# A first block of 128 rows on half a batch, and mirrored rows added on VectorE in three batches

## The chip, the cores and the metric

One core of one Trainium2 chip runs the whole program. The metric is the time of one execution in device microseconds. The inputs, the weights and the result lie in the chip's memory; nothing is kept from one execution to the next.

## The reference, cut to what matters

Eight batches of 2496 tokens with 256 features go through a two-dimensional Fourier transform of which only the real part is kept. Each transformed token is then routed to one of eight experts, a two-layer network, and is scaled with its gate.

```python
X = np.fft.fft(np.fft.fft(x, axis=1), axis=2).real      # (8, 2496, 256)
x = X.reshape(19968, 256)
logits = x @ w_gate + modality_bias[modality_id]
e_idx = argmax(logits, 1); gate_w = softmax(logits)[e_idx]
for e in range(8):
    h = maximum(x[e_idx == e] @ w1[e], 0)               # 256 -> 1024
    out[e_idx == e] = gate_w * (h @ w2[e])              # 1024 -> 256
```

## The kernel before, in words

**The transform of a batch.** The host lays out each batch as a tile XM in two halves (c = 0 and 1) of five blocks each, and every half holds a plain part (`XM[:, 0]`) and a mirrored part (`XM[:, 1]`); what the transform needs is the sum of the two. Stage 1 (`stage1`, L539 in the batches below) multiplies XM with the constants c1, stage 2 (L570) with the matrices m2u, stage 3 (L585) with e3. Batches 0 to 2 run this in float32, where one matmul stands in the trace as two records; batches 3 to 7 run it in pairs of float16 (L536, L565, L583). Stages 2 and 3 are one generator, `stage23`, of twelve steps. Its results go from PSUM into rows `rp` (ScalarE L516, VectorE L517), and the columns for the gate go into Lg (L593).

**How the mirrored part gets in.** From batch 3 on VectorE adds the two parts first (`fold_add`, L397). In batches 0 to 2 (UB = 3) no add is made: stage 1 has two matmuls for each block, one with the plain and one with the mirrored part, and both add up in PSUM (L539). The sum of squares, from which a power of two for scaling is taken, then needs four passes on ScalarE in a batch (L394) where two would do with the sum (L398).

**Routing.** `route` picks the experts with some twenty small VectorE instructions, counts tokens on TensorE (L669, L671) and makes the row numbers `dsti` (L682). The rows go into a buffer `xd` in the chip's memory, sorted by expert: 11 indirect DMAs of plain rows (`rp`, called plus in the code) and 11 of mirrored rows (`rm`, VectorE L227 and L228) per batch, all issued by GpSimd (L708) one after the other.

**Expert blocks.** `block` takes 256 rows of one expert: SyncE reads the start row from a table (L1064), loads the rows transposed (xT, L1077) with their gates and row numbers (ig, L1080), then come 48 matmuls with w1 (L1096), ScalarE and VectorE into H (L1101, L1102), 48 matmuls with w2 (L1116), ScalarE into `ob` (L1124), and a scatter to the result on GpSimd (L1125). The first GEMM of a block runs ahead of the second GEMM of the block before it. Three lists of blocks with experts fixed in advance (ORDER_S) come first: experts 0, 1, 2 once batch 0 is scattered (`spec_blocks(ORDER_S[0], 1)`), then 13 blocks once batch 1 is scattered, then 8 once batch 2 is. A table on VectorE (`spec_table`) gives the start row, or empty rows where an expert has too few tokens. The other blocks follow from tables, and the last ones have 128 rows.

**Weights.** Each expert has two units of weights, w1 (even) and w2 (odd), 1 MB each. A unit is loaded (`wload`, L826), folded on VectorE if it is w1 (L834, L835), measured (L848 on TensorE), split into a high half on ScalarE (`whi`, L869) and a low half on VectorE (`wlo`, L876), and stored for later (`wstore`, L883). Units 0 to 5 are called by hand between steps of the batches, in the main function.

**What sets the order.** The program is written as generators that are stepped by hand (`steps`, `ORDER0`, `ORDER1`, SPOS). A scheduler then gives each engine one fixed order by priority: what is written earlier comes first unless its inputs are late by the scheduler's own clock; then later work is pulled ahead. `issue_after(x)` places an instruction behind x, `behind(f, x)` does so at lower priority, and `high_priority` pulls ahead. Each engine and each queue then runs in its fixed order, so an instruction that waits holds up everything behind it.

Of the kernel before, what the change touches and what calls it, by code (L numbers as in the profile page):

```python
# [22 lines left out]
P = 128  # L23
# [50 lines left out]
UB = 3  # L74
RV = 1
FG = 6
ORDER_S = (0, 1, 2), (0, 1, 2, 3, 3, 4, 4, 5, 5, 6, 6, 7, 7), (5, 6, 7, 0, 1, 2, 3, 4)
# [166 lines left out]
class Kernel:  # L244
# [116 lines left out]
    def scatter_dep(self, ins, b):  # L361
# [24 lines left out]

    def fold_add(self, b, c):
        n = 4 if b < UB else 2
        if c == 0:
            self.sq = self.fft.tile([P, n], F32, name=f"nst{n}")  # L390
        if b < UB:
            jk = self.wp.tile([P, NH * D], F16, name="xj", bufs=1)
            for h in range(2):
                self.nc.scalar.activation(jk.rearrange("p (i d) -> p i d", i=NH), self.XM[c][:, h], AF.Square, accum_out=self.sq[:, 2 * c + h:2 * c + h + 1])  # L394
# [60 lines left out]
    def scale(self, b):  # L455
# [7 lines left out]
        self.pow2(self.total(self.sq, self.psf.tile([P, 512], F32, name="psf")), eb, s, 204 if b >= FB else 188, 2.0 if b < UB else 1.0)  # L463
# [8 lines left out]
    def fold(self, b, c):  # L472
# [11 lines left out]
        if b < UB:  # L484
            self.PQ = self.XM[c][:, :, :, 0:P], self.XM[c][:, :, :, P:D]
# [33 lines left out]
    def stage1(self, b, c):  # L519
# [3 lines left out]
        for h, src in enumerate(self.PQ):  # L523
# [3 lines left out]
            for i0, n in ((0, 3), (3, 2)):  # L527
# [4 lines left out]
                for i in range(n):  # L532
# [4 lines left out]
                    elif b < UB:  # L537
                        for k in range(2):
                            self.staged = nc.tensor.matmul(o, src[:, k, i0 + i, :], self.c1[:, i1 + i, :], start=k == 0, stop=k == 1).ins  # L539
                    else:  # L540
                        nc.tensor.matmul(o, src[:, i0 + i, :], self.c1[:, i1 + i, :], start=True, stop=True)
# [83 lines left out]
    def route(self, b):  # L625
# [49 lines left out]
        V.tensor_tensor(nbase, ps[:, 176:184], self.base, ALU.add)  # L675
        self.base = self.bases[b + 1] = nbase
# [17 lines left out]
        for i, group in enumerate(groups):  # L694
            if b < 2:
# [3 lines left out]
                for x in group.list:  # L699
                    self.scatter(*x)  # L700
# [6 lines left out]
    def scatter(self, row, at, b):  # L707
# [3 lines left out]
        self.scatter_dep(i, b)  # L711
# [31 lines left out]
    def stream(self):  # L743
# [13 lines left out]
        for b in range(B):  # L757
# [4 lines left out]
            for g, _ in enumerate(self.stage23(b)):  # L762
# [3 lines left out]
                if g == 0 and b + 1 == FB:  # L766
                    self.m2_split()
# [5 lines left out]
                yield self.at(b)  # L773
            if b + 1 == FB:
# [545 lines left out]
```

## Time and profile before

| | us |
|---|---|
| median of 3 runs (lowest to highest) | 1033.86 (1032.04 to 1037.51) |
| the profiled execution, its own time | 1035.88 |
| its span, first to last instruction | 1034.1 |
| busy TensorE / VectorE / ScalarE / GpSimd | 1000.7 / 540.5 / 443.5 / 367.6 |

The profiled execution is 2.0 above the median, and 1.8 of it lie outside the span. TensorE is busy for 97% of the span, so the time is its work plus some 33 us in which it waits, and about half of that lies in the first 200 us, where the change is.

### The profile page before, as it was taken

Reading aid. Unit: us, or ns where it says so; the run is one execution under the profiler, and the core shown is the slowest. Engines: PE = TensorE matmul, PEld = TensorE weight load, DVE = VectorE, ACT = ScalarE, POOL = GpSimd, SP = SyncE. Lnnn points to the kernel's source line nnn. Section 1 sums busy time; section 2 is a strip of 40 time slices with the busy share of each in tenths; the row PEclk is TensorE's granted clock in tenths of the full one; section 3 lists DMA queues with packets and bytes.
Section 4 is the critical chain, followed back from the end, with each engine's and each line's share of the span. In section 5 each row is a group of like instructions: output and inputs, shape, how many; then the busy total and the mean of one; then the engine's idle time right before and its main releaser. Section 6 shows DMA issues by size and latency. Waiting matters only on the chain.

```text
span 1034.1 us, 25844 instructions
## 1 busy us (share of the span) xinstructions
PE 1000.7 (97%) x9910; PEld 904.4 (87%) x9910; DVE 540.5 (52%) x1577; ACT 443.5 (43%) x870; POOL 367.6 (36%) x351
## 2 busy tenths in 40 slices
PE   6989899999999999999999999999999999999996
PEld 6878788898998889999999998888888888889896
DVE  2859866576857558779754347423232322222221
ACT  4775566555643354455533333333232323233232
POOL 0077822135414441744344334335351212121111
PEclk9999999999999999999999999999999999999999
DMA  9837969278558958989766963897788895594891
GB/s 327 332 137 234 363 167 287 58 236 249 166 139 284 321 157 236 287 250 304 233 182 200 248 184 76 260 262 241 174 235 235 255 257 175 159 294 137 225 207 35
DMA packets 149725, 227.65 MB, mean 220 GB/s; under 512 B 116309, under 2 KB 117375, under 8 KB 132695
## 3 DMA queue, kind: packets, MB, share of 16 engines
q1 hardware_dynamic: 133031, 183.75, 61.1%
q0 software_dynamic: 16560, 42.15, 11.8%
q8 instruction: 80, 1.31, 0.5%
q14 instruction: 54, 0.44, 0.2%
HBM read 191.77 MB, written 62.48 MB: 246 GB/s over the span
## 4 chain that ended last, share of the span: by engine, by line
PE 69%; issue 12%; DMA 10%; POOL 4%; DVE 2%; ACT 2%; SPq 1%; POOLq 0%; ACTq 0%
PE psm L1096 30%; PE pso L1116 30%; DMA wa<-w 5%; DMA XM<-x 3%; POOL out L1125 3%; PE psf L565 2%; PE psf L583 2%; PE psf L570 2%; PE psf L536 1%; POOL xd L708 1%; PE psf L585 1%; DMA pack<-c_pack 1%; PE psf L539 1%; DMA xT<-xd 1%; DVE w L876 1%
## 5 line engine op out<-in xcount | busy, mean ns | idle before, releaser
L1096 PE MATMUL psm<-xT,w 128*128 128x256 f16 (+1 forms) x4368 | 454.4, 261 | 10.2 <-DVE H L1102 5.8
L1116 PE MATMUL pso<-w,H 128*128 128x256 f16 x3864 | 450.5, 273 | 0.9 <-ACT ob L1124 0.9
L1096 PEld LDWEIGHTS <-w 128*128 128x128 f16 x4368 | 384.3, 98 | 49.9 <-issue 8.4
L1116 PEld LDWEIGHTS <-H 128*128 128x128 f16 x3864 | 375.3, 98 | 43.7 <-issue 1.1
L1102 DVE SCALAR_TENSOR_TENSOR H<-psm,H 128x512 f16<-128x512 f32 x322 | 219.8, 687 | 334.6 <-ACT H L1101 334.0
L1125 POOL DMA_INDIRECT out<-ob,ig x161 | 164.7, 1023 | 516.9 <-ACT ob L1124 486.8
L1101 ACT ACTIVATE H<-psm 128x512 f16<-128x512 f32 x322 | 190.5, 596 | 229.9 <-PE psm L1096 227.1
L1124 ACT ACTIVATE ob<-pso,gs 128x256 f32<-128x256 f32 x161 | 68.6, 471 | 247.0 <-PE pso L1116 207.5
L708 POOL DMA_INDIRECT xd<-rp,dsti x88 | 101.4, 1152 | 94.3 <-DVE rm L228 49.9
L708 POOL DMA_INDIRECT xd<-rm,dsti x88 | 92.9, 1055 | 41.9 <-issue 18.5
L517 DVE SCALAR_TENSOR_TENSOR T<-psf,T 120x280 f16<-120x280 f32 (+2 forms) x95 | 43.4, 463 | 42.3 <-ACT T L516 42.2
L876 DVE SCALAR_TENSOR_TENSOR w<-wa,wsc,w 128x1024 f16<-128x1024 f32 x32 | 39.9, 1276 | 9.4 <-ACT w L869 9.3
L516 ACT ACTIVATE T<-psf 120x280 f16<-120x280 f32 (+2 forms) x95 | 38.8, 422 | 10.5 <-PE psf L536 5.7
L570 PE MATMUL psf<-m2u,T 128*120 128x280 f32 x132 | 37.2, 403 | 2.2 <-DVE Lg L593 1.5
L539 PE MATMUL psf<-c,XM 128*128 128x132 f32 x240 | 31.5, 294 | 7.0 <-DMA c<-c_c 6.9
L539 PEld LDWEIGHTS psf<-c,XM 128*128 128x128 f32 x240 | 30.4, 204 | 7.1 <-DMA XM<-x 6.9
L583 PE MATMUL psf<-T,pack 120*128 120x145 f16 x330 | 34.7, 224 | 1.5 <-DVE T L517 1.5
L869 ACT ACTIVATE w<-wa,wsc 128x1024 f16<-128x1024 f32 (+1 forms) x24 | 33.4, 1425 | 4.3 <-DVE wsc L405 3.5
L565 PE MATMUL psf<-pack,T 128*120 128x144 f16 (+1 forms) x330 | 31.5, 229 | 0.0
L512 ACT COPY T<-psf 120x280 f32<-120x280 f32 (+2 forms) x57 | 22.7, 407 | 17.1 <-PE psf L570 8.2
L855 ACT ACTIVATE xj<-wa 128x1024 f16<-128x1024 f32 x20 | 21.1, 1054 | 18.0 <-DVE wa L834 9.1
L516 ACT ACTIVATE rp<-psf 128x256 f16<-128x256 f32 x55 | 21.1, 383 | 15.8 <-PE psf L583 11.8
(186 smaller groups left out, 598.0 us busy)
## 6 DMA issues: line engine op xcount, KB each, us to landing
w<-w SPq DMA_DIRECT2D x80, 1028.0 KB
w<-w SPq DMA_DIRECT2D x80, 1024.0 KB
XM<-x SPq DMA_DIRECT2D x14, 1280.0 KB
wa<-w SPq DMA_DIRECT2D x16, 1024.0 KB
out<-ob,ig POOLq DMA_INDIRECT x161, 7.1
XM<-x SPq DMA_DIRECT2D x2, 768.0 KB
xT<-xd SPq DMA_TRANSPOSE x91
xd<-rp,dsti POOLq DMA_INDIRECT x88, 5.2
```

What stands on the lines that cost most here:

```text
L516: self.acted = self.nc.scalar.activation(dst[:, 0], ps, AF.Identity, scale=scale).ins
L539: self.staged = nc.tensor.matmul(o, src[:, k, i0 + i, :], self.c1[:, i1 + i, :], start=k == 0, stop=k == 1).ins
L565: nc.tensor.matmul(oh, T1[h][:, a, g, :], self.m2h[h][:, w], start=h + k == 0, stop=h * k == 2, skip_group_check=True)
L570: nc.tensor.matmul(ps[0:120, 0:280], T1[h][:, g, :], self.m2u[h], start=h == 0, stop=h == 1)
L583: nc.tensor.matmul(ps3[0:P, cols], self.e3h[:, a, j, :], T2[:, w, cols], start=k == 0, stop=k == 2)
L708: i = self.nc.gpsimd.indirect_dma_start(out=self.t["xd"], out_offset=bass.IndirectOffsetOnAxis(ap=at, axis=0), in_=row, in_offset=None, bo ...
L1096: l1 = nc.tensor.matmul(ps[:, q, :], w1v[:, h, kt, ft], xT[:, xs, :], start=k == 0, stop=k == 5).ins
L1101: nc.scalar.activation(H[:, 0, f0:f0 + NF, :], ps, AF.Relu)
L1102: self.mark = V.scalar_tensor_tensor(H[:, 1, f0:f0 + NF, :], ps, 0.0, H[:, 0, f0:f0 + NF, :], ALU.max, ALU.subtract).ins
L1116: nc.tensor.matmul(po[:, tg, :], H[:, hh, ft, tg * P:(tg + 1) * P], w2v[:, wh, ft, :], start=k == 0, stop=k == 23)
L1124: self.ob = nc.scalar.activation(ob, po[:, tg, :], AF.Identity, scale=gs[:, tg:tg + 1]).ins
L1125: ins = nc.gpsimd.indirect_dma_start(out=t["out"], out_offset=bass.IndirectOffsetOnAxis(ap=ig.bitcast(I32)[:, tg, 0:1], axis=0), in_=ob, i ...
```

## The change

It has six parts.
1. The mirrored half is added on VectorE in batches 0 to 2 too: batch 0 in four pieces as the data come (PARTS), batches 1 and 2 in two adds that are placed behind steps 7 and 9 of the `stage23` of the batch before (ADDS). Stage 1 then has one matmul for a block and the sum of squares two passes.
2. A block of 128 rows of expert 0 is run on the plain rows of batch 0 alone (HALF, `spec_table` with R = 0.5), after the first half of stage 1 of batch 2; it doesn't wait for mirrored rows (group xd_m0).
3. The first list has blocks of 128 rows, experts 0, 1, 1, 2, 2 where it had 0, 1, 2 of 256.
4. `whi`, `wlo`, `wstore` of unit 1 and the load of unit 5 come after routing of batch 0.
5. `m2_split` (the float16 copies of m2) moves from the `stage23` of batch 2 to behind that of batch 0.
6. Squares of both halves of batches 1 and 2 are called together at step f.

```diff
+ADDS = 7, 9
+HALF = (0,)
-ORDER_S = (0, 1, 2), (0, 1, 2, 3, 3, 4, ...
+ORDER_S = (0, 1, 1, 2, 2), (0, 1, 2, 3, 3, 4, ...
...
-        tc.add_to_no_dep_group(f"xd_w{b}", i)
+        tc.add_to_no_dep_group("xd_m0" if mirrored and b == 0 else f"xd_w{b}", i)
...
-        for b in range(self.nread, B):
+        if self.nread < 1:
+            tc.declare_no_dep(i, group="xd_m0", reason="only the plain rows are read")
+        for b in range(math.ceil(self.nread), B):
...
+    def add(self, c, *parts):
+        for i0, i1 in parts or ((0, NH),):
+            X = self.XM[c][:, 0, i0:i1]
+            self.nc.vector.tensor_tensor(X, X, self.XM[c][:, 1, i0:i1], ALU.add)
...
     def fold_add(self, b, c):
...
-        if b < UB:
-            jk = self.wp.tile([P, NH * D], F16, name="xj", bufs=1)
-            for h in range(2):
-                self.nc.scalar.activation(jk..., self.XM[c][:, h], AF.Square, ...)
-            return
         X = self.XM[c][:, 0]
-        self.nc.vector.tensor_tensor(X, X, self.XM[c][:, 1], ALU.add)
+        if b >= UB:
+            self.add(c)
+        elif b == 0:
+            self.add(c, *PARTS)
         self.nc.scalar.activation(self.XM[c][:, 1], X, AF.Square, accum_out=self.sq[:, c:c + 1])
...
-                    elif b < UB:
-                        for k in range(2):
-                            self.staged = nc.tensor.matmul(o, src[:, k, i0 + i, :], self.c1[:, i1 + i, :], ...)
                     else:
-                        nc.tensor.matmul(o, src[:, i0 + i, :], self.c1[:, i1 + i, :], start=True, stop=True)
+                        self.staged = nc.tensor.matmul(o, src[:, i0 + i, :], self.c1[:, i1 + i, :], ...).ins
...
+        if b == 0:
+            hb = rt.tile([1, 8], F32, name="hbase", bufs=1)
+            V.tensor_tensor(hb, ps[0:1, 8 * G:8 * G + 8], self.base[0:1, :], ALU.add)
+            self.bases[0.5] = hb
...
-                if g == 0 and b + 1 == FB:
-                    self.m2_split()
+                if b + 1 < UB and g in ADDS:
+                    with self.tc.issue_after(self.mark):
+                        self.add(ADDS.index(g))
...
+            if b == 0:
+                with self.tc.issue_after(self.acted), self.tc.issue_after(self.mark):
+                    self.m2_split()
...
-    behind(both(k.whi, 0, 1), k.acted)
-    behind(both(k.wlo, 0, 1))
-    both(k.wstore, 0, 1)()
-    both(k.wload, 4, 5)()
+    behind(both(k.whi, 0), k.acted)
+    behind(both(k.wlo, 0))
+    k.wstore(0)
+    k.wload(4)
     steps(12 - WHI)
     steps(7)
+    behind(both(k.whi, 1), k.expi)
+    behind(both(k.wlo, 1), k.plused, k.head)
+    k.wstore(1)
+    k.wload(5)
...
     steps(5)
+    k.hold = k.staged,
+    run_all([k.spec_blocks(HALF, 0.5, S=P)])
+    run_all([k.prev])
+    k.prev = None
     steps(3 + 1)
...
-    spec = k.spec_blocks(ORDER_S[0], 1)
+    spec = k.spec_blocks(ORDER_S[0], 1, S=P)
```

## Rows read from the trace of the kernel before

**Rows 1.** Windows of two stages: length, busy time (instructions) per engine, clock, DMA.
```profile
41.27:85.63 44.36, 40.88 (x341) 36.15 (x340) 31.61 (x158) 33.16 (x62) 23.94 (x23) 1.00 0.51 173
85.63:136.30 50.67, 46.00 (x364) 39.22 (x363) 42.65 (x112) 30.32 (x61) 42.49 (x27) 0.97 0.89 309
```

**Rows 2.** Windows of L539 alone (stage 1, batches 0, 1, 2): PE, PEld, clock, DMA.
```profile
6.90:18.84 11.94, 11.94 (x80) 11.78 (x80) 1.00 0.98 332
41.27:51.70 10.43, 10.00 (x80) 9.36 (x80) 1.00 0.93 333
75.18:85.63 10.45, 9.38 (x80) 9.04 (x80) 1.00 0.29 81
```

**Rows 3.** Timeline of PE: start, length, instructions [idle before, releaser].
```profile
18.84 0.52 PE L334 MATMUL psf<-awm,pack 128*128 128x16 f32 x4
...
21.75 0.63 PE L848 MATMUL psm<-wa 128*128 128x128 bf16 x8 [0.99 <-DVE wa L834]
22.23 2.09 PE L570 MATMUL psf<-m2u,T 128*120 128x280 f32 x8
...
38.46 0.75 PE L585 MATMUL psf<-T,pack 120*128 120x145 f32 x4 [0.37 <-ACT T L512]
...
61.58 1.17 PE L570 MATMUL psf<-m2u,T 128*120 128x280 f32 x4 [1.45 <-DVE Lg L593]
...
136.30 4.09 PE L1096 MATMUL psm<-xT,w 128*128 128x256 f16 x36 [1.13 <-DMA xT<-xd]
```

**Rows 4.** Groups by form of L397 and of L1096 with 256 and 128 columns.
```profile
L397 DVE TENSOR_TENSOR XM<-XM 128x1280 f32<-128x1280 f32 x10 | 14.9, 1488 | 15.6 <-DMA XM<-x 15.5
...
L1096 PE MATMUL psm<-xT,w 128*128 128x256 f16 x3360 | 394.7, 273 | 7.5 <-DVE H L1102 5.8 <-DMA xT<-xd 1.7
L1096 PE MATMUL psm<-xT,w 128*128 128x128 f16 x1008 | 59.7, 219 | 2.7 <-DMA w<-w 2.7
```

**Rows 5.** Timeline of VectorE.
```profile
50.20 0.18 DVE L682 CAST dsti<-dst 128x22 int32<-128x22 f32 x1
...
53.70 1.21 DVE L834 TENSOR_TENSOR wa<-wa 128x1024 f32<-128x1024 f32 x1
...
82.58 0.10 DVE L682 CAST dsti<-dst 128x22 int32<-128x22 f32 x1
...
84.50 3.65 DVE L876 SCALAR_TENSOR_TENSOR w<-wa,wsc,w 128x1024 f16<-128x1024 f32 x3
...
94.13 0.67 DVE L1102 SCALAR_TENSOR_TENSOR H<-psm,H 128x512 f16<-128x512 f32 x1
```

**Rows 6.** Window from the first dsti to the last Lg of batch 1.
```profile
50.38:76.45 26.07, 23.07 (x176) 18.81 (x174) 15.75 (x76) 18.92 (x36) 19.64 (x19) 1.00 0.42 149
```

**Rows 7.** Timeline of GpSimd, the scatters of batches 0 and 1.
```profile
54.07 1.70 POOL L708 DMA_INDIRECT xd<-rp,dsti  x1 [0.30 <-ACT T L512]
...
65.69 0.97 POOL L708 DMA_INDIRECT xd<-rp,dsti  x1 [0.30 <-ACT T L512]
...
79.75 1.03 POOL L708 DMA_INDIRECT xd<-rm,dsti  x1 [0.30 <-issue]
84.75 10.30 POOL L708 DMA_INDIRECT xd<-rp,dsti  x1 [3.97 <-ACT T L512]
...
127.71 1.41 POOL L708 DMA_INDIRECT xd<-rm,dsti  x1 [0.30 <-issue]
```

**Rows 8.** Timeline of SyncE's queue: start and length of the issue.
```profile
46.04 6.21 SPq L385 DMA_DIRECT2D XM<-x  x2
82.36 1.37 SPq L1077 DMA_TRANSPOSE xT<-xd  x1
...
131.79 1.29 SPq L1077 DMA_TRANSPOSE xT<-xd  x1
```

**Rows 9.** Timeline of ScalarE: a square that waits for batch 2.
```profile
59.11 1.27 ACT L394 ACTIVATE xj<-XM 128x1280 f16<-128x1280 f32 x1 [1.51 <-DMA XM<-x]
```

**Rows 10.** Windows of L570 alone, then of L585 alone, behind the second list's start.
```profile
136.30:180.00 43.70, 2.22 (x8) 1.33 (x8) 1.00 0.81 245
...
136.30:180.00 43.70, 3.15 (x16) 2.44 (x16) 1.00 0.81 245
```

More of the change, by code (lines that the diff above doesn't have):

```diff
@@ L359, in hp, with scatter_dep @@
         return self.tc.high_priority(n) if n else ExitStack()
-    def scatter_dep(self, ins, b):
+    def scatter_dep(self, ins, b, mirrored=False):
         tc = self.tc
@@ L699, in route @@
                 for x in group.list:
-                    self.scatter(*x)
+                    self.scatter(*x, mirrored=True)
             else:
@@ L705, in route, with scatter @@
             yield 1
-    def scatter(self, row, at, b):
+    def scatter(self, row, at, b, mirrored=False):
         i = self.nc.gpsimd.indirect_dma_start(
@@ L710, in scatter @@
             in_=row, in_offset=None, bounds_check=XROWS - 1, oob_is_err=False)
-        self.scatter_dep(i, b)
+        self.scatter_dep(i, b, mirrored)
         self.scattered = i.ins
@@ L784, in stream @@
                     next(s, None)
+                elif step == "f" and b + 1 < UB:
+                    with self.tc.issue_after(self.acted if b == 0 else self.head):
+                        self.fold(b + 1, 0)
+                        self.fold(b + 1, 1)
+                    self.parts(0)
                 elif step == "f":
@@ L796, in stream @@
                         self.bias(b + 1)
-                        if b == 0:
-                            x.enter_context(self.tc.issue_after(self.expi))
-                        self.fold(b + 1, 1)
+                        if b + 1 < UB:
+                            self.parts(1)
+                        else:
+                            self.fold(b + 1, 1)
                     for _ in s:
@@ L903, in spec_table @@
         n = len(visits)
-        row = lambda nm, w=8, dt=F32: rt.tile([1, w], dt, name=f"sp_{nm}{n}", bufs=1)
+        row = lambda nm, w=8, dt=F32: rt.tile([1, w], dt, name=f"sp_{nm}{n}_{S}", bufs=1)
         av = row("av")
@@ L944, in runs, with spec_blocks @@
         return out
-    def spec_blocks(self, visits, nb, resident=None):
-        ti = self.spec_table(visits, nb)
+    def spec_blocks(self, visits, nb, resident=None, S=256):
+        ti = self.spec_table(visits, nb, S)
         for j, e in enumerate(visits):
             self.nread = nb
-            b = self.block(256, ti, j, ex=e, slot=e % 3 if resident is None else (visits[0] + j) % 3, load=resident is not None and j >= resident)
+            b = self.block(S, ti, j, ex=e, slot=e % 3 if resident is None else (visits[0] + j) % 3, load=resident is not None and j >= resident)
             next(b)
@@ L1214, in fft_moe @@
     k.hold = k.staged,
[L1215 removed]
+    spec = k.spec_blocks(ORDER_S[0], 1, S=P)
     next(spec)
[L1217 removed]
+    i, nw, half, step = 1 + len(HALF) / 2 - 0.5, 6, 0, 0.5
     k.slots = lambda b: 2 * sum(len(v) for v in ORDER_S[:b]) - half
@@ L1222, in fft_moe @@
         if n:
-            spec = k.spec_blocks(visits, n + 1, None if n < 2 else 3)
+            spec, step = k.spec_blocks(visits, n + 1, None if n < 2 else 3), 1
         for full in spec:
             if full == 0:
-                i += 1
+                i += step
             else:
-                while nw < 16 and i >= 5 and nw < WEIGHT[min(i - 5, 7)]:
+                while nw < 16 and i >= 5 and nw < WEIGHT[min(int(i) - 5, 7)]:
                     behind(lambda: k.wall(nw))
@@ L1233, in fft_moe @@
                 k.rows = k.pool("rows", 1)
-            x = knots(i - (0.5 if full == 0 else 0), SPOS)
+            x = knots(i - (step / 2 if full == 0 else 0), SPOS)
             half += 1
```

30 lines of the change are left out of this document (14 added, 16 removed).

## The prediction

> **What bounds the kernel now.** I read the windows by stage first, then the timelines of TensorE, VectorE, GpSimd and the SyncE queue for the first 140 us; nothing in the change touches what comes later. In both windows TensorE is the fullest engine: it idles 44.36 − 40.88 = 3.48 us in the first and 50.67 − 46.00 = 4.67 us in the second [rows 1]. So removed TensorE work would come out of the time if nothing else were close. One thing is close. The second list of blocks needs batch 1 scattered. Its first row load is issued at 131.79 [rows 8], behind the last scatter at 127.71 [rows 7], and TensorE waits for it, though for only 1.13 us [rows 3]. Two chains meet at 136.30 almost together: TensorE's own work, and the chain routing of batch 0, `stage23` of batch 1, routing of batch 1, 22 scatters on GpSimd. Whatever shortens only the first leaves TensorE waiting for the second. I therefore work out both.
>
> **TensorE's side, part by part.**
>
> *Stage 1 halved.* Each batch has 80 records, and 40 go. In batch 1 that is 40 × 10.00/80 = 5.0 us, in batch 2 40 × 9.38/80 = 4.7 us [rows 2]. In batch 0 half of 11.94 is 5.97 us, but there the data arrive meanwhile (DMA share 0.98 [rows 2]), and before `stage23` TensorE stands 0.99 us for the first fold of weights (L834) until 21.75 [rows 3]. If that order stays, nothing is gained; if the first L570 goes ahead, up to 5.97. I take 1.5, near the lower end, because the row with the wait is the nearer one.
>
> *The adds.* An add of 1280 columns takes 1.49 us [rows 4]. Six such lengths make 8.9 us of VectorE. Batch 0's third of it lies beside loads; the two adds for batch 1 lie in `stage23` of batch 0 and replace the 2.5 us of `wlo` of unit 1 that leave it; the two for batch 2 lie in `stage23` of batch 1. If VectorE had no room there, 3.0 us would lie on the path. Removing six squares of ScalarE at 1.27 us each [rows 9] costs nothing and shortens no bound engine by itself, but one of them waits 1.51 us for batch 2's data in the middle of batch 1's `stage23` [rows 9], and TensorE waits 1.45 us behind it [rows 3]. The squares now come after `stage23`, so that wait goes: 1.45.
>
> *Unit 1 and m2_split moved.* Unit 1's high half delayed TensorE by 0.37 us in batch 0 [rows 3]; that goes. `m2_split` is under 2 us of small instructions on ScalarE and VectorE; nothing on TensorE waits for it before batch 3. Zero for TensorE as long as VectorE has room (next part).
>
> *Blocks of 128.* With 128 columns a matmul takes 59.7/1008 = 59.2 ns, with 256 394.7/3360 = 117.5 ns [rows 4]. Six blocks of 128 need 288 × 59.2 = 17.05 us, three of 256 need 144 × 117.5 = 16.92 us: +0.1. The rows done are the same: by the reference's own routing experts 0, 1, 2 have 317, 326, 327 tokens in batch 0, and expert 0 has 161 among the plain rows, so no block is empty, before or after. SyncE issues three more row loads at 1.37 us [rows 8], in a stretch where it has few others. The half block runs its second GEMM at once, with no block between: from zero (other work fills) up to one eviction pair, some 1.3 us; I take 0.3.
>
> Sum: 1.5 + 5.0 + 4.7 + 1.45 + 0.37 − 0.1 − 0.3 = 12.6 us less for TensorE up to the second list.
>
> **The scatter chain's side.** Row numbers of batch 0 are ready at 50.38 [rows 5]. Of the gains they get 1.5 + 0.37 = 1.9: routing is a string of dependent VectorE steps that nothing shortens. From there to the last gate columns of batch 1 are 26.07 us, in which VectorE is busy 15.75 and TensorE 23.07 [rows 6]. To VectorE come `wlo` of unit 1 (two of three in 3.65 us [rows 5], 2.4), two adds (3.0) and `m2_split` (under 2): 22.8 to 23. TensorE has its 23.07 less what moves ahead. So this stretch shrinks to about 23, by 3 us, now held by VectorE. Row numbers of batch 1 come 4.9 us earlier, at 77.8.
>
> GpSimd: after batch 1's row numbers VectorE runs without a break from 84.50 to 94.13, and the first scatter takes 10.30 us, from 84.75 until 0.92 us after the first L1102 at 94.13 begins [rows 5, 7]; another takes 0.97 [rows 7]. One beside L834 at 53.70 takes 1.70 [rows 5, 7]. So operations of VectorE with two inputs in SBUF hold a scatter up, by 0.7 us where one stands alone. The Trainium skill (SBUF — State Buffer, on the shared port pair) says that such an instruction contends with a GpSimd instruction that reads SBUF, which agrees; it also infers that an add of two tiles doesn't slow the making of DMA descriptors, and by that the holds would be nought, against these rows. With the rows: `wlo` (2) and adds (2) now fall among batch 0's scatters, +4 × 0.7 = 2.8, and the half block's scatter adds 1.3. Batch 0's last one, 80.78 before [rows 7], ends at 80.78 − 1.9 + 2.8 + 1.3 = 83.0. That is no loss: the first of batch 1 is held until 94.13 − 4.9 = 89.2 anyway. From there everything follows as before, so the second list's rows come 4.9 us earlier, at 131.4 on TensorE.
>
> **The sum.** TensorE could be 12.6 us earlier, the rows only 4.9: 7.7 us of idle would open ahead of the second list. Of work that stood behind 136.30, 2.22 + 3.15 = 5.4 us of batch 2's `stage23` [rows 10] could fill it. The engine order is fixed in advance, so between none and all of it does; I take 3. Gain 4.9 + 3 = 7.9. The profiled execution's 1035.88 becomes 1028.0; the median shown is 2.0 lower, so 1026.
>
> **The rivals.**
>
> *All of it comes out* (0.2). If the hold on GpSimd falls away (the VectorE run is broken up by the earlier blocks' evictions) or float16 stage 1 of batch 3 fills the hole, the gain is the 12.6: 1021. For it: the run is only one string of `wlo`, and a 128-row block evicts beside it. Against: the order of both is unchanged.
>
> *Next to nothing* (0.22). The half block reaches TensorE before its rows. Plain scatters end at 66.66 [rows 7], less 1.9, plus holds of up to 2.8, 67.6; a row load is on TensorE 3.3 us later (82.36 to 85.63 [rows 1, 8]), 70.9. TensorE gets there at 75.18 + 2.35 less 9 (1.9, 5.0 and the rest), 68.5. That is 2.4 us of waiting, and with the start and VectorE's stretch giving nothing the rest is 7.9 − 2.4 − 1.5 − 3 = 1: 1033.
>
> *Slower* (0.13). Batch 2's data are loaded behind unit 5, which now waits for unit 1's `wlo`, after routing; the loads were issued from 46.04 to 52.25 [rows 8], and the second landed at 59.11 [rows 9], 6.9 later. If the queue's fixed order puts the second load behind the half block's row load, which waits for scatters until about 69, it lands near 77. The add for it is due near 64, and VectorE, which takes its instructions in order, holds up every eviction behind it: `stage23` of batch 1 ends some 6 us later than before, the scatter chain with it, and of that little is got back: 1038 to 1040. It decides as soon as the load is issued later than about 62. Against it: by its place in the program the load comes well ahead of the half block.
>
> That a part doesn't do what it says I hold unlikely; the group for mirrored rows would show it, as the first 128-row load would then come after 81.
>
> **How the numbers follow.** The forecast has 0.45 and its own range, by the bounds at the start and of the filling, is 1021 to 1031. The range reaches from the first rival to past the second: 1018 to 1036; it leaves out the slower case and the tails, under 0.2. A measurement of this kernel can tell about 0.5%, 5.2 us, from no change. Faster than 1028.7: 0.2 + 0.38 of the forecast's 0.45 = 0.58. Slower than 1039: half of the third rival and tails, 0.09. The rest, 0.33, is within.
>
> **What would show it.** Right: 120 records of L539, near 15 us; dsti of batches 0 and 1 at 48 and 78; the first 128-row load near 68; a scatter of some 10 us behind dsti of batch 1; the second list's first matmul near 131 with several us of idle ahead. Wrong: that idle absent (first rival); TensorE waiting for xT before 75 (second); an add that waits for XM by more than 5 us (third); idle that opens behind 136, which I count at none.

## The result, and the profile after

| | before | after |
|---|---|---|
| median of 9 runs each, one chip (us) | 1034.16 | 1040.66 |
| lowest to highest | 1032.04 to 1037.53 | 1038.69 to 1044.47 |
| ratio, 95% interval | | 1.0065 [1.005, 1.0081] |
| profiled execution, its span | 1035.88, 1034.1 | 1043.17, 1041.3 |

The change is slower by 6.5 us; 1026 was predicted, 1036 was the upper end of the range, and 0.09 stood on slower. The profiled execution of after lies 2.5 above its median, that of before 1.7. Where single runs stood out as slower, the ratios leave them out; the medians are of all runs.

Windows of after: the first 200 us, then the two stages of [rows 1], then the stretch of [rows 6].
```profile
0.00:200.00 200.00, 171.85 (x1444) 149.25 (x1445) 139.44 (x450) 114.21 (x220) 72.97 (x63) 0.95 0.76 242
...
41.39:88.90 47.51, 39.45 (x304) 34.33 (x304) 34.34 (x169) 30.48 (x58) 26.61 (x22) 0.89 0.54 162
88.90:144.66 55.76, 47.15 (x452) 40.83 (x452) 44.74 (x126) 29.47 (x59) 35.31 (x26) 0.94 0.91 285
48.88:79.37 30.49, 23.27 (x153) 18.55 (x152) 20.96 (x94) 15.55 (x30) 23.76 (x20) 0.94 0.68 230
```
Windows of after with stage 1 alone (L548, which was L539), as [rows 2]: PE, PEld, clock, DMA.
```profile
6.00:18.59 12.59, 7.01 (x40) 6.30 (x40) 0.96 0.98 338
41.39:52.00 10.61, 7.14 (x40) 6.48 (x40) 0.84 0.04 13
75.50:88.90 13.40, 7.00 (x40) 6.29 (x40) 0.87 0.45 74
```
The window of the first 200 us of before:
```profile
0.00:200.00 200.00, 182.58 (x1493) 160.55 (x1494) 133.37 (x426) 124.09 (x236) 77.23 (x65) 0.99 0.73 245
```
Its expert matmuls in these 200 us, as groups by form (count, busy us, mean ns, idle before):
```profile
L1096 PE MATMUL psm<-xT,w 128*128 128x256 f16 x443 | 53.5, 276 | 4.4 <-DVE H L1102 3.3 <-DMA xT<-xd 1.1
L1116 PE MATMUL pso<-w,H 128*128 128x256 f16 x384 | 45.8, 273 | 0.3 <-ACT ob L1124 0.3
```
The same groups of after, first 200 us:
```profile
L1135 PE MATMUL pso<-w,H 128*128 128x256 f16 x340 | 40.6, 276 | 0.0
...
L1115 PE MATMUL psm<-xT,w 128*128 128x256 f16 x276 | 32.1, 273 | 0.0
...
L1115 PE MATMUL psm<-xT,w 128*128 128x128 f16 x288 | 18.4, 224 | 1.5 <-DMA xT<-xd 1.4
```

**The whole loss is there by 200 us.** Before had then done 443 matmuls of 256 columns on L1096 and 384 on L1116, 827; after has done 276 + 340 and 288 of half the size, 760. The missing 67 at 117.5 ns [rows 4] are 7.9 us; the spans differ by 7.2.

**The matmuls went, the time did not.** The 120 records that are gone took half of [rows 2], 15.7 us. TensorE is only 10.7 us less busy (182.58 − 171.85), which is 10.7 us more of waiting. For 7.9 us less of progress and 15.7 less to do it should have been busy for 182.58 − 15.7 − 7.9 = 159.0. The other 12.9 us are the same records running longer. By groups of these 200 us stage 1 is 5.4 of it and the same 264 matmuls of `stage23` 4.5: the 40 of batch 1 take 7.14 us, not 5.00, at a granted clock of 0.84 on average, those of batch 2 7.00, not 4.69, at 0.87. These means are of two levels: from 42 to 44 us the granted clock is 0.50 (1.2 GHz), from 46 to 60 it is 1.00 (2.4 GHz). The lower one stands in this trace behind waits of TensorE (0.76 and 1.30 us ahead of 41.49, 4.66 ahead of 65.71, 1.93 ahead of 79.02), but not behind each (not behind 1.44 at 89.50). The Trainium skill (TensorE: Matmul & The Clock Gate, Part 1) has the same two levels and the fall after idling; these stretches agree. By the mean clock of the 200 us, 0.95 against 0.99, the clock makes some 7 of the 12.9 us, an estimate; no view here accounts for the rest.

The timeline of TensorE, after; L577, L592, L676 and L1115 were L570, L585, L669 and L1096:
```profile
18.59 3.27 PE L577 MATMUL psf<-m2u,T 128*120 128x280 f32 x8
...
39.73 0.36 PE L427 MATMUL psf<-mst,ones 128*128 128x1 bf16 x2 [0.76 <-ACT pack L438]
41.39 0.16 PE L427 MATMUL psf<-nst,ones 128*128 128x1 bf16 x1 [1.30 <-ACT XM L408]
...
65.71 1.30 PE L592 MATMUL psf<-T,pack 120*128 120x145 f32 x4 [4.66 <-ACT T L522]
...
79.02 3.42 PE L548 MATMUL psf<-c,XM 128*128 128x132 f32 x14 [1.93 <-DVE Lg L600]
82.23 2.90 PE L1115 MATMUL psm<-xT,w 128*128 128x128 f16 x48
...
85.00 0.24 PE L676 MATMUL psf<-oh,tri 128*128 128x176 f16 x1
...
89.50 0.77 PE L1115 MATMUL psm<-xT,w 128*128 128x128 f16 x11 [1.44 <-DMA xT<-xd]
...
119.14 0.16 PE L427 MATMUL psf<-wst,ones 128*128 128x1 bf16 x1 [4.58 <-ACT xj L874]
...
133.16 0.16 PE L427 MATMUL psf<-wst,ones 128*128 128x1 bf16 x1 [2.60 <-ACT xj L874]
...
144.66 4.09 PE L1115 MATMUL psm<-xT,w 128*128 128x256 f16 x36
```
VectorE, after: row numbers of batch 0 (50.20 in [rows 5]), the last gate columns of batch 1, its row numbers (82.58 in [rows 5]), a fold of weights.
```profile
48.70 0.18 DVE L693 CAST dsti<-dst 128x22 int32<-128x22 f32 x1
...
79.18 0.16 DVE L600 COPY Lg<-psf 128x16 f32<-128x16 f32 x1
...
88.86 0.16 DVE L693 CAST dsti<-dst 128x22 int32<-128x22 f32 x1
...
116.68 1.23 DVE L853 TENSOR_TENSOR wa<-wa 128x1024 f32<-128x1024 f32 x1 [5.86 <-DMA wa<-w]
```
SyncE's queue, after (as [rows 8]): unit 4 and 5, batch 2's data, the half block's rows, two loads of weights, the first list's last rows, the second list's first.
```profile
34.83 20.30 SPq L845 DMA_DIRECT2D wa<-w  x2
...
55.72 1.84 SPq L390 DMA_DIRECT2D XM<-x  x2
...
72.98 1.31 SPq L1096 DMA_TRANSPOSE xT<-xd  x1
...
97.75 1.74 SPq L845 DMA_DIRECT2D wa<-w  x2
...
103.91 4.17 SPq L845 DMA_DIRECT2D wa<-w  x2
...
113.06 7.22 SPq L1096 DMA_TRANSPOSE xT<-xd  x1
136.62 1.83 SPq L1096 DMA_TRANSPOSE xT<-xd  x1
```
The same two loads of weights before:
```profile
92.33 1.46 SPq L826 DMA_DIRECT2D wa<-w  x2
...
96.01 2.75 SPq L826 DMA_DIRECT2D wa<-w  x2
```
GpSimd, after (as [rows 7]):
```profile
52.56 4.16 POOL L719 DMA_INDIRECT xd<-rp,dsti  x1 [0.30 <-ACT T L522]
...
89.80 0.97 POOL L719 DMA_INDIRECT xd<-rp,dsti  x1 [6.96 <-issue]
...
124.95 0.97 POOL L719 DMA_INDIRECT xd<-rm,dsti  x1 [0.30 <-issue]
```
The chain of work that ended last, after: the first of these two until its data have landed.
```profile
52.56 12.23 DMA xd<-rp,dsti
```
ScalarE, after:
```profile
64.90 0.47 ACT L526 ACTIVATE rp<-psf,xsc 128x256 f16<-128x256 f32 x1 [7.26 <-DMA xd<-rp,dsti]
...
74.66 1.27 ACT L408 ACTIVATE XM<-XM 128x1280 f32<-128x1280 f32 x1
...
75.92 1.99 ACT L888 ACTIVATE w<-wa,wsc 128x2048 f16<-128x2048 f32 x1
```

**Where the row numbers of batch 1 lose 6.3 us.** Up to the start of `stage23` all goes better than forecast: 18.59, where before had 22.23 [rows 3] and 1.5 us of gain were forecast. Row numbers of batch 0 come 1.5 us earlier. Then the load of unit 5 stands on SyncE's queue (the 20.30 us are of units 4 and 5 together, nearly all of them its wait), because its buffer is given back by unit 1's `wlo`. Behind it batch 2's data are asked for at 55.72, not at 46.04 [rows 8], so these 2.6 MB, unit 1's store and batch 0's rows move at once. A scatter at 52.56 needs 4.16 us beside `wlo` on VectorE, and its data land 12.23 us after its start. ScalarE wants to put its next row into that buffer and waits 7.26 us; TensorE stands 4.66 behind it. A square and a weight scaling then run ahead of the last evictions (74.66 to 77.91), for another 1.93. Last, the half block's 48 matmuls (82.23) stand ahead of the matmuls that count tokens (85.00).

**Behind the row numbers.** From there the second list follows after 55.80 us (88.86 to 144.66), against 53.72 before, but not in the same way. Batch 1's first scatter, held for 10.30 us before [rows 7], takes 0.97 at 89.80, and the last starts at 124.95, 2.8 us earlier than before (127.71). The list's first row load comes 11.7 us behind that last start (136.62), where it was 4.1 [rows 7, 8], since SyncE waits for the scattered data to land. And still TensorE comes to the list at 144.66 without a wait, so its own queue ends last. Between 88.90 and 144.66 it waits 8.6 us (before, from 85.63 to 136.30, 4.7), and 7.2 of them lie in two waits for totals of squares of weights (119.14, 133.16). ScalarE's square ahead of the first stands behind the fold that waits 5.86 us for weights at 116.68, and the loads of weights were issued at 97.75 and 103.91 where it was 92.33 and 96.01. By a count of the records done, each at its length before, after is some 1 us of work behind at 90 us, so by then the 15.7 us taken off are used up, and some 8 behind at 137: the loss itself opens here. Both are estimates. The low halves of units 2 and 3 stand behind batch 1's row numbers by program, and the next loads behind them; that the late row numbers reach these waits by that way is argued, and no run tests it.

### The profile page after: what moved, and what is told of

It is laid out like the page before. It is cut to its first block, busy times and chain, and to the rows that moved or that the text cites. A ratio compares the mean times of both kernels' runs of the same rounds, so it can differ in the third digit from the quotient of the medians.

```text
span 1041.3 us, 25927 instructions
## 1 busy us (share of the span) xinstructions
PE 998.0 (96%) x9928; PEld 899.2 (86%) x9928; DVE 549.8 (53%) x1609; ACT 435.8 (42%) x858; POOL 365.0 (35%) x351
## 4 chain that ended last, share of the span: by engine, by line
PE 63%; issue 16%; DMA 10%; POOL 4%; DVE 4%; ACT 1%; SPq 1%; POOLq 0%; ACTq 0%; DVEq 0%
PE psm L1115 27%; PE pso L1135 27%; DMA XM<-x 4%; POOL out L1144 3%; PE psf L577 2%; PE psf L572 2%; PE psf L590 2%; DMA ig<-xd 2%; POOL xd L719 1%; DMA xd<-rp,dsti 1%; DMA out<-ob,ig 1%; PE psf L546 1%; PE psf L592 1%; DMA xT<-xd 1%; DMA wa<-w 1%
## 5 line engine op out<-in xcount | busy, mean ns | idle before, releaser
L1115 PE MATMUL psm<-xT,w 128*128 128x256 f16 (+1 forms) x4512 | 454.3, 258 | 7.0 <-DVE H L1121 3.6
L1115 PEld LDWEIGHTS <-w 128*128 128x128 f16 x4512 | 387.1, 98 | 49.7 <-issue 11.7
L1144 POOL DMA_INDIRECT out<-ob,ig x161 | 166.8, 1036 | 526.2 <-ACT ob L1143 496.0
L719 POOL DMA_INDIRECT xd<-rp,dsti x88 | 95.5, 1086 | 95.7 <-ACT T L522 49.3
L577 PE MATMUL psf<-m2u,T 128*120 128x280 f32 x132 | 40.3, 433 | 0.2
L395 DVE TENSOR_TENSOR XM<-XM 128x1280 f32<-128x1280 f32 (+2 forms) x18 | 24.1, 1337 | 24.5 <-DMA XM<-x 24.5
L577 PEld LDWEIGHTS psf<-m2u,T 128*120 128x120 f32 x132 | 23.9, 198 | 8.8 <-DVE web L414 2.8
L548 PE MATMUL psf<-c,XM 128*128 128x132 f32 x120 | 21.1, 339 | 9.8 <-DVE XM L395 7.9
L548 PEld LDWEIGHTS psf<-c,XM 128*128 128x128 f32 x120 | 19.1, 242 | 12.7 <-DVE XM L395 7.4
```

The source lines that it names most:

```text
L548: self.staged = nc.tensor.matmul(o, src[:, i0 + i, :], self.c1[:, i1 + i, :], start=True, stop=True).ins
L577: nc.tensor.matmul(ps[0:120, 0:280], T1[h][:, g, :], self.m2u[h], start=h == 0, stop=h == 1)
L719: i = self.nc.gpsimd.indirect_dma_start(out=self.t["xd"], out_offset=bass.IndirectOffsetOnAxis(ap=at, axis=0), in_=row, in_offset=None, bo ...
L1115: l1 = nc.tensor.matmul(ps[:, q, :], w1v[:, h, kt, ft], xT[:, xs, :], start=k == 0, stop=k == 5).ins
L1144: ins = nc.gpsimd.indirect_dma_start(out=t["out"], out_offset=bass.IndirectOffsetOnAxis(ap=ig.bitcast(I32)[:, tg, 0:1], axis=0), in_=ob, i ...
```

## The experiments

Two theories came from this trace: **A**, the early unit 1 (part 4) blocks SyncE's queue and makes the row numbers late; **B**, the half block does (part 2). Later ones are told where they come. All times are medians, with the ratio to the kernel before on the same chip. In the tables "dsti" is the start of L693 (L682) for batches 0 and 1 and "second list" that of its first matmul, in the profiled execution.

**Undoing one part.** e1 has unit 1 back, e2 one more row buffer (against the wait of 7.26), e3 no half block, e4 only the adds and the moved split.

```diff
e1: -    behind(both(k.whi, 1), k.expi) ... k.wload(5)
    +    behind(both(k.whi, 0, 1), k.acted) ... both(k.wload, 4, 5)()
e2: -RPB = 5
    +RPB = 6
    -            jk = p.tile([P, NH * D], F16, name="xj", bufs=1)[:, 0:F]
    +            jk = p.tile([P, F], F16, name="xj", bufs=1)
e3: -ORDER_S = (0, 1, 1, 2, 2), ...
    +ORDER_S = (0, 0, 1, 1, 2, 2), ...
    -    run_all([k.spec_blocks(HALF, 0.5, S=P)])
e4: the edit of e1, ORDER_S = (0, 1, 2) in blocks of 256, no half block
```


> Undone: part 4 alone (high and low half, store of unit 1 and load of unit 5 stand where they stood before). Theory A (the load of unit 5, held for 20 us in SyncE's queue, lets it, the store of unit 1 and batch 2's data all start at 55 and run against batch 0's scatters; a scatter lands 8 us late, its row buffer is not free, ScalarE stands 7.26 us): that wait falls below 2 us, batch 2's loads are issued near 46, row numbers of batch 1 come near 82 instead of 88.9, and the time falls by 5 to 8 us, to 1033 to 1036. Rival B (the half block ahead of the counting matmuls is what delays row numbers of batch 1): they come at 86 or later, time 1038 or more.

> One more row buffer (RPB 6 instead of 5; a scratch tile of ScalarE is 512 bytes smaller to make room), all else as in the changed kernel. Theory A: the loads still start at 55, but the step that waited has a free buffer; the wait for a scatter shrinks from 7.26 us to 3 or less, row numbers of batch 1 come 3 to 5 us earlier, time 1036 to 1038. If the wait is for the bulk transfers in another way than through the buffer, nothing changes: 1040 to 1041.

> Undone: the half block alone; the first list has six blocks of 128 (experts 0, 0, 1, 1, 2, 2) behind all of batch 0. Theory A: ScalarE's wait of 7 us for a scatter stays, row numbers of batch 1 come 2 to 3 us earlier as the counting matmuls no longer stand behind 48 matmuls, time 1037 to 1040. Rival B: 1033 to 1036.

> Undone: parts 2, 3 and 4; what is left is the adds with half the matmuls, the squares called together and the earlier m2 split. Theories A and B both: no wait of over 3 us on ScalarE for a scatter, row numbers of batch 1 near 78, second list near 131, time 1026 to 1031, which is the forecast's sum without the two parts that spoiled it. Rival C (VectorE's load by the adds is what costs): 1036 or more.

| | us | ratio [95%] | dsti 0, 1 | second list |
|---|---|---|---|---|
| before (beside e1 to e4: 1034.75) | 1034.2 | | 50.2, 82.6 | 136.3 |
| after | 1040.7 | 1.0065 [1.005, 1.0081] | 48.7, 88.9 | 144.7 |
| e1 unit 1 back | 1057.3 | 1.0219 [1.0189, 1.0248] | 49.5, 115.3 | 156.9 |
| e2 six row buffers | 1053.7 | 1.0178 [1.0149, 1.0206] | 48.9, 112.7 | 153.5 |
| e3 no half block | 1049.5 | 1.0145 [1.0109, 1.0182] | 48.7, 86.7 | 146.1 |
| e4 adds and split only | 1043.3 | 1.0076 [1.0047, 1.0105] | 50.2, 82.2 | 136.5 |

A and B fail on the time: no undoing made it faster, and e1, e2 and e3 are clearly slower than the change. What held were rivals' numbers: B's in e1 (row numbers at 86 or later, 1038 or more), and in e4 the 1036 or more of VectorE's load (named C there; further down **C** is another theory). But VectorE isn't full in e4's windows below. In e1 ScalarE's wait of 7.26 us is gone and the counting matmuls come at 80.66 instead of 85.00, as A has it, and yet the row numbers are 26 us later. GpSimd shows part of it (timeline of e1):
```profile
102.41 0.97 POOL L1144 DMA_INDIRECT out<-ob,ig  x1 [20.40 <-ACT ob L1143]
115.69 1.34 POOL L719 DMA_INDIRECT xd<-rp,dsti  x1 [12.32 <-DVE rm L211]
```
The scheduler fixes each engine's order anew for each program. Here it put the half block's result ahead of batch 1's rows on GpSimd, and on VectorE the low halves of units 2 to 5, an add that waits for data (5.85 us) and a fold that waits for weights (5.05) ahead of the row numbers. The same order came out in e2. So these two say little of the part that they undo.

e4 says most. It has the adds and no half block, no early unit, no blocks of 128, and is as slow as the whole change. Its row numbers and its second list stand where they stood before (82.2 and 136.5). What was taken off TensorE came back as waiting. Windows of before, 12 us:
```profile
68.00:74.00 6.00, 5.53 (x32) 4.17 (x30) 2.43 (x12) 5.71 (x10) 4.53 (x5) 1.00 0.27 95
74.00:80.00 6.00, 5.84 (x48) 5.55 (x49) 4.91 (x18) 5.64 (x8) 4.47 (x6) 1.00 0.24 83
```
The same windows of e4:
```profile
68.00:74.00 6.00, 3.55 (x24) 2.85 (x22) 3.30 (x10) 6.00 (x10) 4.78 (x5) 1.00 0.20 69
74.00:80.00 6.00, 2.79 (x16) 2.17 (x15) 4.07 (x17) 6.00 (x9) 4.78 (x5) 0.85 0.29 101
```
And the timeline of e4's TensorE:
```profile
89.64 6.80 PE L1115 MATMUL psm<-xT,w 128*128 128x256 f16 x36 [6.23 <-DMA xT<-xd]
```
ScalarE is busy without a break from 68 to 80: the squares of batch 2, which before lay at 52.26, 53.79, 59.11 and 61.10, can run only after the adds, and there they meet the scaling of units 2 and 3. Then (last row) the first list's rows are not there before 89.64, since batch 0's scatters on GpSimd end no earlier than before (the last starts at 81.77, before at 79.75). In the whole of 40 to 90 TensorE waits 13.2 us, against 3.5 before, and its clock falls to 0.88. Yet less than half of e4's loss is there by 200 us: it has then done 803 matmuls of 256 columns where before has 827, and by 300 us 1553 against 1609, that is 2.8 and 6.6 us at 117.5 ns. Why more than half of it opens after 200 us is open.

**Holding the order fixed.** **D** stands in the expectations from here on for the rival that the removed matmuls weren't on the path and come back as waits and half clock, or that the row numbers alone set the list. **C** was that the tags of a 128-row block (ig, four buffers), given back only by result scatters, hold SyncE's queue. e5 tests that alone. e6 is e1 with the row numbers forced ahead of the weights on VectorE; e7 adds C's buffers and puts the half block's result behind batch 1's rows; e8 also has the split of m2 back in batch 2.

```diff
e5: -        ig = p.tile([P, NT, 2], F32, name=f"ig{S}", bufs=4)
    +        ig = p.tile([P, NT, 2], F32, name=f"ig{S}", bufs=8 if S == P else 4)
e6: the edit of e1, and
    -    behind(both(k.wlo, 2, 3), k.plused)
    +    behind(both(k.wlo, 2, 3), k.plused, k.head)
    the same for units 4, 5
e7: e6, e5, and the half block's result issued after k.scattered of batch 1
e8: e7, and m2_split() where it was before
```


> The changed kernel with eight instead of four buffers for the tags (ig) of a 128-row block; the order of GpSimd's queue and VectorE's up to the second list stay. Theory C (the tags' four buffers are given back only by result scatters that stand behind batch 1's rows on GpSimd, so SyncE stands at the fifth block's tags, 12.5 us at the longest, and the second list's rows are loaded late): that wait goes, the second list begins near 139 to 141 instead of 144.66, and the time is 1035 to 1038 us. Rival D (the second list waits for batch 1's rows, which follow the row numbers at 88.86, whatever SyncE does): the list begins within 2 us of 144.66, 1039 to 1042 us.

> Unit 1 of the weights goes back beside unit 0, as in e1_unit1_back, and the low halves of units 2 to 5 are told to wait for batch 1's row numbers, so that VectorE's queue has the row numbers first. Theory A (the early unit 1 holds SyncE's queue, its loads land among the scatters, and this is 4.35 us of the row numbers' delay): counting matmuls near 80.7, row numbers of batch 1 at 83 to 84.5 instead of 88.86, time 1033 to 1037 us; the 16 us that e1_unit1_back lost beyond that were the order of VectorE's queue. Rival B (the half block and ScalarE's queue hold the row numbers): not before 87, time 1038 us or more.

> As e6_unit1_order, with the half block's result scattered only behind batch 1's 22 row scatters and with eight buffers for the tags of 128-row blocks. Theories A and C together: the row numbers as in e6, batch 1's rows go out unbroken in 28 to 32 us from there, the second list begins at 134 to 138, time 1027 to 1033 us. Rival D (the matmuls taken away were not on the path, they come back as waits and half clock): the second list begins no earlier than before the change (136.3), and the time is 1033 us or more.

> As e7_order_late_ig8, with the splitting of m2 put back into batch 2. Theory M (the split's total stands in TensorE's queue at 39.7 and costs 0.76 and 1.30 us of waiting, after which the granted clock falls): these waits go, the row numbers of batch 0 come 1 to 2 us earlier, the clock in 40 to 50 stays above 0.95, and the time is 2 to 4 us below e7. Rival (the waits only move to the next one, where ScalarE's queue ends last at 68 to 80): within 1 us of e7.

| | us | ratio [95%] | dsti 0, 1 | second list |
|---|---|---|---|---|
| e5 tags | 1043.3 | 1.0081 [1.0057, 1.0106] | 49.0, 89.8 | 144.9 |
| e6 unit 1 back, order held | 1044.1 | 1.0081 [1.005, 1.0111] | 51.5, 85.3 | 147.9 |
| e7 and late result, tags | 1048.6 | 1.0128 [1.009, 1.0167] | 51.7, 85.5 | 148.2 |
| e8 and split back | 1044.95 | 1.0094 [1.0062, 1.0125] | 50.5, 85.7 | 147.5 |

C falls: e5 changes nothing. e6 takes 13 us off e1, so that much of e1 was the order. A is right in direction on the row numbers, which come 3.6 us earlier than in the change (at 85.3, with 83 to 84.5 expected), and wrong on the time: the second list starts 3.3 us later, with TensorE waiting for the first list's rows (timeline of e6):
```profile
125.04 1.25 PE L1115 MATMUL psm<-xT,w 128*128 128x128 f16 x10 [8.53 <-DMA xT<-xd]
```
In e8 the split's wait is gone, and the wait for the square behind it grows from 1.30 to 1.81 us. On the same chip e8's median lies 3.7 us under e7's, as its theory had it (2 to 4), but the clock in 40 to 50 is 0.83, not above 0.95, and the intervals overlap: that the moved split costs this much isn't settled.

**Row buffers (G), on other chips.** Three row buffers (xT) hold 768 rows in blocks of 256 and 384 in blocks of 128. So the fourth and fifth row load of the first list stand on SyncE's queue between 8 MB of bulk (95.22 and 113.06 in after); before, all three were asked for by 87.15. The next nine runs went to three chips on which the kernel before takes 1083.7 to 1085.0 us; what is different there is told in the last section. Ratios there can be set beside each other, and g1 is the change itself.

```diff
e9, f1: e5, and xT of the first list's fourth and fifth block from two buffers of their own
e10, f3: the kernel before with its first list as (0, 0, 1, 1, 2, 2), S=P
e11, f2: the changed kernel with the doubled matmuls, the squares and the m2_split of before
e12: the changed kernel with ORDER_S = (0, 1, 2) in blocks of 256 and no half block
f4: e6 with the buffers of f1
g1: the changed kernel
```


> The changed kernel with two more buffers for the rows of a 128-row block (the fourth and fifth of the first list) and eight for their tags. Theory G (three row buffers hold 768 rows in blocks of 256 and 384 in blocks of 128, so the fourth and fifth loads stand in SyncE's queue behind 8 MB of bulk loads and stores and land late): all row loads of the first list are issued by 92 us (95.22 and 113.06 in the changed kernel), its last block starts before 128 (138.84), the second list before 141 (144.66), time 1033 to 1037 us. Rival D (the row numbers at 88.86 and what follows them set the second list's start): start of the list within 2 us of 144.66, time 1039 to 1042 us.

> The kernel of e9_xt5 again: the changed kernel with two more row buffers and eight tag buffers for blocks of 128. Theory G: all rows of the first list asked for by 92 us, its last block started before 128 (138.84 in the changed kernel), second list before 141 (144.66), time 1033 to 1037 us where the kernel before takes 1034. Theory D: the second list within 2 us of 144.66, time 1039 to 1042 us.

> The kernel before with one thing of the change: the first list in six blocks of 128 rows instead of three of 256, no half block, nothing else. Theory G: the rows of the fourth to sixth block are issued among the bulk, TensorE waits 5 us or more for rows, tags or weights between 90 and 140, time 1038 to 1045 us. The prediction's term for blocks of 128 (0.1 us less): 1033 to 1036 us.

> The kernel of e10_before_128 again: the kernel before with the first list in six blocks of 128 and nothing else. Theory G: row loads among the bulk, TensorE waits 5 us or more for rows, tags or weights between 90 and 140, 1038 to 1044 us. The prediction's term for blocks of 128 (0.1 us less): 1033 to 1036 us.

> The changed kernel with the doubled matmuls back (parts 2, 3 and 4 without the adds and the moved split). Theory D (what costs is that TensorE's work went, as waiting and half clock): the granted clock in 40 to 90 is back above 0.97 and the time is 1030 to 1035 us. Theory G (what costs are the blocks of 128): 1037 to 1044 us.

> The kernel of e11_no_adds again: the half block, the blocks of 128 and the early unit 1 with the doubled matmuls back. Theory D: the work that fills TensorE also keeps its clock, so granted clock above 0.97 in 40 to 90 and 1032 to 1036 us, faster than the change though it does 120 matmuls more. Theories A and G: row numbers of batch 1 and rows of the first list as late as in the change, 1040 to 1046 us.

> The changed kernel with the first list in three blocks of 256 and without the half block (the adds, the split and the early unit 1 stay). Theory A: against e4_adds_only (1043.3) the early unit 1 makes batch 1's row numbers 4 to 5 us later, time 1046 to 1049 us. Theory G: the row loads stay ahead of the bulk, the second list begins at 141 or earlier, time 1038 to 1043 us.

> e6_unit1_order (unit 1 back beside unit 0, row numbers first on VectorE's queue; 1044.1) with the row and tag buffers of f1_xt5. Theories A and G together: row numbers of batch 1 near 85, the wait of 8.53 us for rows at 125 gone, second list at 136 to 140, 1031 to 1036 us. Theory D: the second list starts early but the time stays at 1037 us or more, since TensorE's waits and half clock between 40 and 90 stay.

> The changed kernel itself. Where the kernel before takes 1034 us: 1040 to 1042 us again. Where it takes 1085 us: by theory G (rows of blocks of 128 behind the bulk) 4 us or more above f1_xt5 and e9_xt5 (ratios 0.9993 and 0.9982), that is a ratio of 1.003 or more; by theory D the same as those two, a ratio of 0.997 to 1.002.

| | us | ratio [95%] |
|---|---|---|
| g1 the change | 1081.2 | 0.9988 [0.9959, 1.0017] |
| e9, f1 with row buffers | 1082.6, 1084.8 | 0.9982 [0.9961, 1.0004], 0.9993 [0.9959, 1.0028] |
| e10, f3 before, blocks of 128 | 1094.0, 1094.6 | 1.0073 [1.0055, 1.009], 1.0078 [1.0054, 1.0102] |
| e11, f2 without the adds | 1085.4, 1088.5 | 1.0004 [0.9978, 1.0029], 1.0042 [1.002, 1.0065] |
| e12 adds, early unit 1, 256 | 1081.4 | 0.9961 [0.9947, 0.9975] |
| f4 unit 1 back, row buffers | 1089.5 | 1.0051 [1.0015, 1.0087] |

On these chips the change makes no difference that can be measured. In f1 the last row load of the first list is issued at 104.45, in g1 at 124.87, and the second list starts at 158.17 and 156.22: the rows come 20 us earlier and nothing follows. G falls as the cause of the late list, there; on the first chips it wasn't tried. But blocks of 128 alone on the kernel before cost 0.73 and 0.78 per cent, twice. That it is through late rows isn't shown: between 90 and 140 the waits of e10's TensorE that have a name are 0.3 us for rows and 1.3 for a total of weights, where G had 5 or more. Nor do the adds cost here what they cost on the first chips: without them, e11 and f2 have 1.0004 and 1.0042, g1 with them 0.9988, and e12 0.9961. Their clocks don't test D, which wanted above 0.97 in 40 to 90 without the adds: it is 0.75 and 0.83 there, and 0.77 in g1.

**The adds alone, on a chip like the first.** g2 is e4 with the split of m2 back in batch 2.

> Only the adds of the change (first list in blocks of 256, no half block, unit 1 beside unit 0, split of m2 in batch 2 as before). Theory D (the matmuls taken away were not on the path): no gain; where the kernel before takes 1034 us, 1036 to 1044 us, the waits of 0.76 and 1.30 us at 39.7 to 41.4 partly gone; where it takes 1085 us, a ratio of 0.995 to 1.002. Rival (the adds bring the forecast's 7.9 us once nothing stands in their way): a ratio of 0.993 or less.

1047.7 us, ratio 1.0135 [1.0113, 1.0158], row numbers at 50.1 and 82.1, second list at 135.5, and TensorE waits 4.88 us for the first rows until 89.73. It loses more than the change (their intervals don't touch), and more than D had (1036 to 1044). The intervals of e4 and g2 don't touch either, if only just, and e4 with the moved split is 0.6 per cent nearer to before: the move is no cost beside the adds, though e8 against e7 points the other way. How much of the 0.6 is the split itself and how much a changed order wasn't tried.

In both, batch 1's scatters come earlier and nothing comes of it (GpSimd and SyncE of e4):
```profile
114.96 0.97 POOL L719 DMA_INDIRECT xd<-rm,dsti  x1 [0.30 <-issue]
```
```profile
132.00 1.29 SPq L1096 DMA_TRANSPOSE xT<-xd  x1
```
This is the last of the scatters, 12.8 us ahead of before's (127.71 [rows 7]); in g2 it is at 115.28. The second list's first row load stands where it stood (131.79 [rows 8]). SyncE now waits 25.1 us for the table of start rows, which VectorE finishes at 130.18 (before 123.05) behind a fold that waits 1.24 us for weights, and TensorE comes to the list at 136.50 without a wait.

## Why the prediction was wrong, point by point

- **"12.6 us less for TensorE up to the second list."** The count of records was right (120), the price wrong, and this step failed for the time itself: e4 and g2, with the row numbers where they stood before, lose too. The start gave 3.6, not 1.5. Stage 1 of batches 1 and 2 gave 10.00 − 7.14 = 2.9 and 9.38 − 7.00 = 2.4, not 5.0 and 4.7, because the remaining records run at the lower clock for part of the time. That what is left can run slower behind new waits stood nowhere in the sum. Over the whole span 15.7 us of matmuls went, 13.0 came back as longer records and 9.9 as waiting (busy 998.0 where it was 1000.7, waiting 43.3 where it was 33.4).
- **The step on the row numbers: "So this stretch shrinks to about 23, by 3 us, now held by VectorE."** 30.49 us, where 23 were forecast and before had 26.07. VectorE was busy for 20.96 of it and isn't what ended last; that was a row buffer, given back by a scatter whose data landed after 12.23 us, and then ScalarE's queue. The prediction took a scatter's time on GpSimd (0.97 to 1.70, with the hold of VectorE) and not the time until its data have landed and the row buffer is free. In e1 and e6, with unit 1 back, ScalarE no longer waits for a scatter's data, and the counting comes 4.3 us earlier in e1; in e2, with one more buffer, that wait is gone too. All three have another order on the engines as well.
- **"Row numbers of batch 1 come ... at 77.8."** 88.86. Of the 11.1 us some 7.5 are the stretch (30.49 against 23); the rest is mostly routing, 9.5 us from the last gate columns where it was 6.1, since the half block's 2.90 us stand ahead of the counting. e3 without it has 86.7.
- **"`m2_split` ... nothing on TensorE waits for it before batch 3."** Its total is a matmul: TensorE waited 0.76 us for it at 39.73 and 1.30 for the square behind. A mis-sized term of 2 us, though by e4 against g2 the move was no loss as a whole (e8 against e7 leans the other way).
- **"Blocks of 128 ... +0.1."** The matmuls cost little more than that (18.4 us for 288, 17.05 forecast). The rows of the fourth and fifth block are asked for among the bulk instead of ahead of it. The blocks alone, on the kernel before, cost 0.7 to 0.8 per cent where it was measured, by which way isn't shown; what they cost in the change wasn't tried on the first chips.
- **"From there everything follows as before."** 55.8 us against 53.7 look near, but by luck. The hold of 10 us on the first scatter is absent, the scatters are done 2.8 us earlier than before with row numbers 6.3 later, their data land later, and TensorE is late by itself, behind two totals of weights and the lower clock. So that the late row numbers carry 6.3 of the 8.4 us by which the list is late isn't shown.
- **The rivals.** All of it comes out: its condition, that the hold on GpSimd falls away, came true (0.97 at 89.80), and so did its sign, no idle ahead of the second list; but that list starts at 144.66, near 131 was forecast, and its price failed with the 12.6. Rows that reach TensorE too late for the half block: it ran at 82.23 without waiting, so this falls. The slower case, 1038 to 1040, had the size and the place (unit 5's load waits for unit 1's `wlo`, batch 2's data behind it), but its price was an add that waits for data, and no add waited; the data, asked for at 55.72, met the scatters instead. By its own bound (62) it should not have decided, so its number is near by luck.
- **What holds for the whole.** e4 and g2 show that on these chips the adds by themselves gain nothing and lose 0.8 and 1.4 per cent. The second list stays at 136 although the scatters end 12 us earlier, as a table on VectorE and TensorE's own queue take over, and TensorE's free time becomes waiting and slower records: in e4 11.6 and 12.0 us over the span, for 15.7 removed. Forecast was that 4.9 us come out of that chain and 3 are filled. That the half clock and ScalarE's full stretch (68 to 80) turn "no gain" into a loss is read from e4's windows, and most of its loss opens later; no run kept TensorE busy there to test it, so the cause of the loss is argued, not shown. Why e1 is slower than the change is shown (order, by e6); why e3, e6 and e8, with earlier row numbers, gain nothing on it stays open; from 88 to 150 TensorE waits in them 5.4, 10.9 and 8.0 us for rows.
- No version ran faster than both kernels on the first chips; e12 did so against the kernel before on the others, by 0.4 per cent.

## What to carry to other kernels

Work taken off the busiest engine counts only up to where the next chain stands, and what is left of it may run at half clock after the new waits: price a removed matmul at nothing until the wait that ends last in its stage has moved. Follow a buffer to the moment when the data that leave it have landed, and each queue past every load that waits in it. Where a scheduler fixes the order, compare the orders of two versions before comparing their times.

## What the hardware showed that was not expected

The same program, the kernel before, took 1034.2 to 1035.0 us in the comparisons on the first chips and 1083.7 to 1085.0 on three others. On the latter, engines stand for several us behind releasers that the profile can't name. The timeline of g1's TensorE:
```profile
74.91 0.72 PE L592 MATMUL psf<-T,pack 120*128 120x145 f32 x4 [2.86 <-remote]
```
The timeline of f3's ScalarE:
```profile
77.04 0.47 ACT L516 ACTIVATE rp<-psf,xsc 128x256 f16<-128x256 f32 x1 [14.09 <-remote]
83.37 0.39 ACT L512 COPY T<-psf 120x280 f32<-120x280 f32 x1 [5.85 <-remote]
```
Batch 1's row numbers come at 101 to 106.5 us there in all nine runs, against 82 to 90 in after, e3 to e8 and g2. The verdict differs with it: 1.0065 on the one kind, 0.9988 on the other. What holds the engines up there is open.

A scatter beside two-input VectorE work took 4.16 us (52.56) where one alone takes 0.97, with `wlo` on VectorE from 52.19 on. The Trainium skill (SBUF — State Buffer, on the shared port pair) says that the loser of that lock waits for the whole instruction; the two `wlo` here take 2.46 together, so by that rule 4.16 us is a wait through more than one instruction. But the length of VectorE's run doesn't set the price: later in after, scatters pass in 0.97 and 2.02 us beside five `wlo` in a row (92.34 to 98.42), where before's took 10.30 beside three and more (84.50, 84.75 [rows 5, 7]). What does is open. The time to land was in no forecast: 12.23 us with 2.6 MB of batch 2 under way.
